# A first-layer matmul in place of an unread one, a weight load in two pieces, and the last output tile as 384 and 128 columns

## Chip, cores, metric

One core of one Trainium2 chip. The metric is the device time of one execution in microseconds. An execution is repeated several times on a chip, in rounds beside the kernel before; single executions of one kernel differ by 0.4 to 1.8 us within a set here (with two further outliers, 509.71 and 510.44), which is more than anything this change can do. In the profiles PE is TensorE (PEld its weight loads), DVE is VectorE, ACT ScalarE, POOL GpSimd and SP SyncE.

## The reference, cut to what matters

```python
# per batch (8) and head (8), sequence 1024, head size 64, projected to 64 rows
k_proj = einsum('ks,bhsd->bhkd', E, k);  v_proj = einsum('ks,bhsd->bhkd', F, v)
attn = softmax(q @ k_proj.T / sqrt(64)) @ v_proj
x = attn, heads side by side: (8192, 512)
h = x @ w_in                      # 512 -> 2048, "first layer"
g = h * clip(h + 3, 0, 6) / 6
out = g @ w_out                   # 2048 -> 512, "second layer"
```

## The kernel before

Only the parts that the change and the argument touch; `...` marks cuts.

```python
def busy(n):                       # matmuls on ones; nobody reads them
    ps = pmm()
    for _ in range(n):
        nc.tensor.matmul(ps, ones[:, :P], ones, start=True, stop=True)
busy(12)
...
for j in range(KO):                # first batch: k and q, then v, pair of heads by pair
    load_pair("k", j); load_q0(0, slice(2 * j, 2 * j + 2))
...
for j in range(KO):
    load_pair("v", j)
...                                # all of these are issued by GpSimd, one queue
for lo, n in ((0, 128), (128, 128), (256, 256), (512, 256), (768, 256),
              (1024, 512), (1536, 512)):
    load_w_in(lo, n)
load_q0(1, slice(0, H))
...                                # w_out in four quarters
load_kqv(1, "kvq")                 # the second batch
...
# end of First.first_block(), the first batch's first half
            self.vals(2, nc.vector.tensor_copy)
            products(1)
            busy(1)
            products(2)
            self.vals(3, nc.scalar.copy)   # project the last pair of v, copy out of PSUM
            busy(1)                        # unread, while ScalarE copies
            products(3)                    # values of the last pair, then xT on VectorE
...
two_groups(xT, 0, g[0], ((0, 1, 2), (3,)))   # first layer, groups 0 and 1
for fo in range(2, FO):
    first_group(xT, 0, g[0], fo)
...
two_groups(xT, 1, g[1], ((0, 1), (2, 3)))
for fo in range(2, FO):
    first_group(xT, 1, g[1], fo)
    pop()
    if fo == 7:
        second.projected()         # second batch: project k and v, matmuls taking turns
...
# second_group(): store of a finished row block
        o_sb = opool.tile([P, d_model], f32, tag="o_sb", name="o_sb")
        (copy or nc.scalar.copy)(o_sb, o_ps)
        nc.sync.dma_start(out=o_dst, in_=o_sb)
```

Each first-layer group is four matmuls of 512 columns (one for each quarter of the contraction), an ACTIVATE on ScalarE and a product on VectorE. The last output tile is cut in two halves of 256 columns, so that the first leaves while the second is computed.

The softmax here doesn't subtract the row's maximum and nothing guards it: scores larger than these inputs give would overflow.

## Time and profile before

| | kernel before |
|---|---|
| time, median of the first 3 runs | 507.60 us (507.38 to 507.77) |
| span of the profiled run | 505.97 us |
| last pair of v: PE starts its projection | 19.73 us, after a wait for the load |
| first product of the first layer on VectorE | 23.39 us |
| PE starts the last output tile | 499.02 us |
| from there to the end | 6.95 us |

Between the first product of the first layer and the last tile, the same instructions run in the same order in before and after. If one kernel is 0.4 us ahead at both points it has lost nothing in between, and if its lead shrinks, the place where it shrinks is a wait. I call the difference of the start of the same instruction in two kernels its **lead**. The lines of the profile stand in the prediction below.

### The profile page before, as it was taken

What the parts mean: (1) busy time and instruction counts of PE and PEld (TensorE: products, weight loads), DVE (VectorE), ACT (ScalarE), POOL (GpSimd) and SP (SyncE); (2) the same over time, 40 slices, a digit from 0 to 9 for tenths busy, and PEclk for the clock granted to TensorE, in tenths of its full rate; (3) what the DMA queues carried; (4) which work ended last, traced back from release to release, by engine and by line L of the source; (5) the groups of instructions that cost most, each with busy time, mean ns of one, the idle gap of its engine ahead of it and who ended that gap; (6) DMA issues with size and microseconds to landing.
All of it is one profiled execution on the core that took longest, in us unless ns stands there. A gap on an engine that the chain in (4) does not pass through costs nothing.

```text
span 506.0 us, 7034 instructions
## 1 busy us (share of the span) xinstructions
PE 495.5 (98%) x2729; PEld 225.1 (44%) x2779; DVE 245.1 (48%) x384; ACT 256.3 (51%) x438; POOL 37.9 (8%) x57
## 2 busy tenths in 40 slices
PE   8899999999999999999999999999999999999997
PEld 4444444444444444444444444444444444444444
DVE  3582736865733564536635455533752446334420
ACT  3656466567564444654555544654455544434431
POOL 8610020020020020010002000000000000000000
PEclk9999999999999999999999999999999999999999
DMA  9999999599299988699317990248110361101112
GB/s 166 199 205 207 202 157 234 109 149 199 79 152 193 264 149 172 137 159 251 113 43 134 216 263 26 63 97 209 41 43 32 79 162 43 41 22 42 43 42 84
DMA packets 77530, 66.04 MB, mean 131 GB/s; under 512 B 36200, under 2 KB 66664, under 8 KB 77496
## 3 DMA queue, kind: packets, MB, share of 16 engines
q0 software_dynamic: 31952, 29.36, 37.1%
q1 hardware_dynamic: 45320, 35.82, 27.0%
q10 hardware_dynamic: 224, 0.39, 0.3%
q8 instruction: 22, 0.36, 0.3%
q14 instruction: 12, 0.10, 0.1%
HBM read 69.73 MB, written 16.94 MB: 171 GB/s over the span
## 4 chain that ended last, share of the span: by engine, by line
PE 94%; DMA 2%; POOL 2%; issue 1%; ACT 1%; DVE 0%; ACTq 0%; POOLq 0%
PE mm L530 43%; PE mm L497 43%; PE at L195 2%; DMA v<-in_v_dram 2%; PE at L244 1%; PE at L226 1%; PE mm L244 1%; PE mm L522 1%; POOL q L106 1%; PE mm L264 1%; POOL k L110 1%; ACT aT L235 0%; PE mm L226 0%; POOL v L110 0%; PE mm L195 0%
## 5 line engine op out<-in xcount | busy, mean ns | idle before, releaser
L503 DVE SCALAR_TENSOR_TENSOR g<-r,mm 128x512 bf16<-128x512 f32 x256 | 173.6, 687 | 179.1 <-ACT r L502 178.3
L497 PE MATMUL mm<-xT,w_in_sb 128*128 128x512 bf16 x998 | 229.2, 379 | 1.5
L530 PE MATMUL mm<-w_out_sb,g 128*128 128x512 bf16 x985 | 227.8, 379 | 1.9 <-issue 1.0
L502 ACT ACTIVATE r<-mm 128x512 f32<-128x512 f32 x256 | 152.3, 599 | 74.5 <-PE mm L497 73.2
L497 PEld LDWEIGHTS <-w_in_sb 128*128 128x128 bf16 x1024 | 99.6, 98 | 121.8 <-issue 3.3
L530 PEld LDWEIGHTS <-g 128*128 128x128 bf16 x1008 | 96.7, 98 | 120.5 <-issue 7.4
L535 ACT COPY o_sb<-mm 128x512 f32<-128x512 f32 x55 | 32.3, 587 | 126.6 <-PE mm L530 126.6
L257 DVE TENSOR_TENSOR xT<-at,rec 128x512 bf16<-128x512 f32 x42 | 26.5, 682 | 6.5 <-ACT rec L176 6.5
L235 ACT ACTIVATE aT<-at 128x512 bf16<-128x512 f32 x38 | 20.2, 615 | 9.1 <-PE at L226 9.1
L201 DVE CAST kp<-at 64x512 bf16<-64x512 f32 x12 | 7.7, 677 | 15.5 <-PE at L195 15.5
L216 POOL COPY mark<-qT 1x1 bf16<-1x1 bf16 x4 | 0.7, 176 | 161.2 <-DMA qT<-q 161.2
L235 ACT ACTIVATE aT<-mm 128x512 bf16<-128x512 f32 x18 | 10.3, 613 | 3.6 <-PE mm L226 3.6
L535 DVE COPY o_sb<-mm 128x512 f32<-128x512 f32 x8 | 5.5, 688 | 13.4 <-PE mm L530 13.4
L195 PE MATMUL at<-k,e_t 128*64 128x512 bf16 x48 | 11.5, 382 | 0.0
L195 PE MATMUL at<-v,f_t 128*64 128x512 bf16 x48 | 11.5, 382 | 0.0
L257 DVE TENSOR_TENSOR xT<-mm,rec 128x512 bf16<-128x512 f32 x14 | 9.0, 685 | 4.3 <-PE mm L244 4.3
L176 ACT ACTIVATE rec<-rec 128x1024 f32<-128x1024 f32 x10 | 10.6, 1060 | 0.3
L170 ACT ACTIVATE rec<-mm 128x512 f32<-128x512 f32 x10 | 5.5, 595 | 7.9 <-PE mm L244 5.4
L170 ACT ACTIVATE few<-mm 128x512 f32<-128x512 f32 x10 | 5.4, 595 | 7.4 <-PE mm L264 7.4
L93 PE MATMUL mm<-ones 128*128 128x512 bf16 x18 | 7.4, 546 | 1.5 <-DVE halves L84 1.5
L204 DVE CAST vp<-at 64x512 bf16<-64x512 f32 x12 | 8.3, 694 | 0.4
L195 PEld LDWEIGHTS <-e_t 128*64 128x64 bf16 x56 | 5.6, 109 | 6.6 <-issue 1.9
(75 smaller groups left out, 160.5 us busy)
## 6 DMA issues: line engine op xcount, KB each, us to landing
out_dram<-o_sb SPq DMA_DIRECT2D x63, 256.0 KB, 2.5
rec<-rows SPq DMA_DIRECT2D x40, 256.0 KB, 6.3
k<-in_k_dram POOLq DMA_DIRECT2D x7, 1024.0 KB, 14.9
v<-in_v_dram POOLq DMA_DIRECT2D x7, 1024.0 KB, 20.7
q<-in_q_dram POOLq DMA_DIRECT2D x7, 1024.0 KB, 10.6
w_out_sb<-in_moe_w_out_dram POOLq DMA_DIRECT2D x4, 512.0 KB, 16.9
k<-in_k_dram POOLq DMA_DIRECT2D x4, 256.0 KB, 5.5
v<-in_v_dram POOLq DMA_DIRECT2D x4, 256.0 KB, 7.8
```

What stands on the lines that cost most here:

```text
L170: nc.scalar.activation(rec[:, i], den, AF.Ln)
L176: nc.scalar.activation(flat, flat, AF.Exp, scale=-1.0)
L195: nc.tensor.matmul(ps[e * KP:(e + 1) * KP], ef_t[e][:, so, :], kqv[self.b]["kv"[e]][:, :, so, :], start=(so == 0), stop=(so == SO - 1))
L204: nc.vector.tensor_copy(self.vp[a * KP:(a + 1) * KP], self.ps[KP:].rearrange("p (h d) -> p h d", d=D))
L235: nc.scalar.activation(self.aT[j][:, r].rearrange("p a n -> p (a n)"), tiles[r], AF.Exp, scale=scale)
L244: nc.tensor.matmul(tiles[t][c:c + D].rearrange("p (r n) -> p r n", r=2), stationary(r, 2 * j + a), self.aT[j][r:r + KP, :, a, :], start=Tr ...
L257: nc.vector.tensor_mul(self.xT[:, j, t, :], av[t], rec[:, t])
L497: nc.tensor.matmul(h_ps, w_in_sb[:, ko, fo * P:(fo + 1) * P], xT[:, ko, t, :], start=(ko == 0), stop=(ko == KO - 1))
L502: nc.scalar.activation(r, h_ps, AF.Relu, bias=0.5, scale=1.0 / 6.0)
L503: nc.vector.scalar_tensor_tensor(g[:, fo, :], r, 1.0, h_ps, op0=ALU.min, op1=ALU.mult)
L530: nc.tensor.matmul(o_ps, g[:, fo, c * P:(c + 1) * P], w_out_sb[:, fo, :], start=(fo == 0), stop=(fo == FO - 1))
L535: (copy or nc.scalar.copy)(o_sb, o_ps)
```

## The change

Intent: PE has a hole of half a microsecond while ScalarE copies the last pair of v, filled with an unread matmul. Let a matmul of the first layer do that duty. Load a later part of w_in in two pieces so that the earlier PE finds it there. At the end, make the piece that leaves last smaller.

```diff
-                  (1024, 512), (1536, 512)):
+                  (1024, 256), (1280, 256), (1536, 512)):
...
             self.vals(3, nc.scalar.copy)
-            busy(1)
+            meanwhile()
             products(3)
...
-            for e, copy, dma in ((0, nc.vector.tensor_copy, nc.sync), (1, nc.scalar.copy, nc.scalar)):
-                half = slice(e * d_model // 2, (e + 1) * d_model // 2)
+            most = d_model * 3 // 4
+            for piece, copy, dma in ((slice(0, most), nc.vector.tensor_copy, nc.sync),
+                                     (slice(most, d_model), nc.scalar.copy, nc.scalar)):
...
+    early = []
+    def meanwhile():
+        early.append(TwoGroups(xT, 0, g[0]))   # allocates the two PSUM tiles
+        early[0].part(0, (0,))                 # group 0, first quarter of the contraction
...
-    two_groups(xT, 0, g[0], ((0, 1, 2), (3,)))
+    early[0].part(0, (1, 2))
+    early[0].part(1, (0, 1, 2))
+    for fo in range(2):
+        early[0].part(fo, (3,))
+    early[0].out()
```

More of the change, by code (lines that the diff above doesn't have):

```diff
@@ L423, in values, with first_block @@
             return self.quads(lambda r, h: self.vp[r:r + KP, h, :], t, j, alloc)
-        def first_block(self):
+        def first_block(self, meanwhile):
             recs = {}
@@ L516, in second_group @@
         if (b, t, c) == (B - 1, NB - 1, SB - 1):
-            for e, copy, dma in ((0, nc.vector.tensor_copy, nc.sync), (1, nc.scalar.copy, nc.scalar)):
-                half = slice(e * d_model // 2, (e + 1) * d_model // 2)
-                o_ps = pmm()[:, :d_model // 2]
+            most = d_model * 3 // 4
+            for piece, copy, dma in ((slice(0, most), nc.vector.tensor_copy, nc.sync),
+                                     (slice(most, d_model), nc.scalar.copy, nc.scalar)):
+                n = piece.stop - piece.start
+                o_ps = pmm()[:, :n]
                 for fo in range(FO):
-                    nc.tensor.matmul(o_ps, g[:, fo, c * P:(c + 1) * P], w_out_sb[:, fo, half],
+                    nc.tensor.matmul(o_ps, g[:, fo, c * P:(c + 1) * P], w_out_sb[:, fo, piece],
                                      start=(fo == 0), stop=(fo == FO - 1))
-                o_sb = opool.tile([P, d_model], f32, tag="o_sb", name="o_sb")[:, :d_model // 2]
+                o_sb = opool.tile([P, d_model], f32, tag="o_sb", name="o_sb")[:, :n]
                 copy(o_sb, o_ps)
-                dma.dma_start(out=o_dst[:, half], in_=o_sb)
+                dma.dma_start(out=o_dst[:, piece], in_=o_sb)
             return
@@ L547, with __init__, part, parts @@
     first = First(xT)
-    first.first_block()
-    x_next = x_tile()
-    g = [g_tile(), g_tile()]
-    def two_groups(xT, t, g, kos):
-        tiles = [pmm(), pmm()]
-        for part in kos:
-            for fo in range(2):
-                h_part(tiles[fo], xT, t, fo, part)
-        for fo in range(2):
-            h_out(tiles[fo], g, fo)
-    two_groups(xT, 0, g[0], ((0, 1, 2), (3,)))
+    g = [g_tile(), g_tile()]
+    class TwoGroups:
+        def __init__(self, xT, t, g):
+            self.xT, self.t, self.g = xT, t, g
+            self.tiles = [pmm(), pmm()]
+        def part(self, fo, kos):
+            h_part(self.tiles[fo], self.xT, self.t, fo, kos)
+        def parts(self, *kos):
+            for some in kos:
+                for fo in range(2):
+                    self.part(fo, some)
+            self.out()
+        def out(self):
+            for fo in range(2):
+                h_out(self.tiles[fo], self.g, fo)
+    early = []
+    def meanwhile():
+        early.append(TwoGroups(xT, 0, g[0]))
+        early[0].part(0, (0,))
+    first.first_block(meanwhile)
+    x_next = x_tile()
+    early[0].part(0, (1, 2))
+    early[0].part(1, (0, 1, 2))
+    for fo in range(2):
+        early[0].part(fo, (3,))
+    early[0].out()
     for fo in range(2, FO):
@@ L579 @@
             (first.second_scores, first.second_sums, first.second_values)[i]()
-    two_groups(xT, 1, g[1], ((0, 1), (2, 3)))
+    TwoGroups(xT, 1, g[1]).parts((0, 1), (2, 3))
     for fo in range(2, FO):
@@ L644 @@
                     if fo == 0:
-                        two_groups(xT, t, g, ((0, 1, 2), (3,)))
+                        TwoGroups(xT, t, g).parts((0, 1, 2), (3,))
                 else:
```

## The prediction

> **What bounds the kernel now.** I read the page first (busy table and chain of waits by line), then the chain of waits in order of time for the first 45 us, then the timeline of 19.7 to 21.3 us and of the last 12 us, then the landings of the loads.
>
> ```profile
> span 506.0 us, 7034 instructions
> PE 495.5 (98%) x2729; PEld 225.1 (44%) x2779; DVE 245.1 (48%) x384; ACT 256.3 (51%) x438; POOL 37.9 (8%) x57
> PE 94%; DMA 2%; POOL 2%; issue 1%; ACT 1%; DVE 0%; ACTq 0%; POOLq 0%
> ```
>
> PE is busy in 98% of the span and is 94% of the chain that ended last. Between 60 us and the end, the view of the waits has for PE only these two:
>
> ```profile
> PE mm L530 <- issue: 1.0, 6, 0.2
> PE mm L530 <- DVE g L503: 0.2, 1, 0.2
> ```
>
> So behind the first stage the program is one row of matmuls that waits for nothing of weight: what is taken from PE's row early comes off the end, and a transfer that merely comes sooner is worth nothing. What can be won lies at the head, where PE waits for loads, in the number of matmuls, and behind the last matmul. The head, from the chain in order of time (start, duration, what):
>
> ```profile
> 9.70 9.99 DMA v<-in_v_dram
> 19.68 0.05 issue
> 19.73 0.63 PE at L382 x8
> 20.36 0.02 issue
> 20.39 0.27 ACT vp L385
> 20.66 0.04 issue
> 20.70 0.40 PE at L414 x2
> 21.11 10.25 PE mm L497 x47
> ```
>
> The last pair of the first batch's v lands; eight matmuls project it (L382), ScalarE copies it out of PSUM (L385), two matmuls multiply it with the attention weights (L414), and then the first layer of the MLP runs (L497). PE has a hole in this chain from the projection's end of issue (about 20.15) to 20.70, while ScalarE copies. In that hole stands now a matmul on ones that nobody reads; the timeline shows its weight load, and the product that finishes xT on VectorE:
>
> ```profile
> 20.13 0.10 PEld L93 LDWEIGHTS <-ones 128*128 128x128 bf16 x1
> 21.22 0.69 DVE L443 TENSOR_TENSOR xT<-at,o_sb 128x512 bf16<-128x512 f32 x1 [1.21 <-PE at L414]
> ```
>
> The tail, from the timeline (start, duration, engine, line, operation):
>
> ```profile
> 499.02 3.66 PE L522 MATMUL mm<-w_out_sb,g 128*128 128x256 bf16 x32
> 501.03 0.42 DVE L525 COPY o_sb<-mm 128x256 f32<-128x256 f32 x1 [14.30 <-PE mm L522]
> 501.48 0.33 SPq L526 DMA_DIRECT2D out_dram<-o_sb  x1
> 502.76 0.37 ACT L525 COPY o_sb<-mm 128x256 f32<-128x256 f32 x1 [2.91 <-PE mm L522]
> 503.16 0.35 ACTq L526 DMA_DIRECT2D out_dram<-o_sb  x1
> ```
>
> The first half leaves early and its landing (2.0 us after issue) is at 503.5; the second is issued at 503.16, lands 1.8 us later at 504.96, and about 1.0 us of closing follows to 506.0. So the end hangs on the second piece.
>
> **What the Trainium skill says.** (1) "TensorE: Matmul & The Clock Gate", Back-to-back issue gap: N/2.4 + 2.5 ns for an isolated stream, but about 81 ns for pairs of weight load and matmul at N=128. The trace sides with the first: sixteen L497 matmuls take 3.45 us in the chain, 216 ns each, and eight 128-column pairs at L382 take 0.62 us of which the last one's latency is 0.219, so (0.62 - 0.219)/7 = 57 ns. (2) "ScalarE: Activation LUTs", What ACT_TABLE_LOAD costs: 186 ns + 0.833 ns per column with immediate operands. The trace has 587 ns at 512 columns, 372 at 256 and 265 at 128: a slope of 0.84, on a base some 25 ns lower. (3) "DMA: Bandwidth & Descriptors", Issuing engines are not separate DMA queues: transfers issued from SP and ACT share the 16 DMA engines. Nothing in the tail shows this yet, since the two pieces hardly overlap there (503.5 against 503.16). (4) The same page, Anatomy of one DMA: a fixed part near 2 us that does not shrink with the size (stated for GpSimd's path). For stores from SP the trace has 2.5 us for 256 KB and 2.0 for 128 KB, so some 1.5 us fixed and 0.25 us per 64 KB.
>
> **Part 1, the early matmul.** It takes away one warm-up matmul (216 ns of PE) and puts one of the first layer's own (first tile, first quarter of the contraction) in its place; later the first layer has one matmul fewer to do. The hole is 0.55 us and either matmul fits in it, so the values still start at 20.70 and the first layer still at 21.04. **Gain: one matmul, 0.216 us**, if nothing that comes 0.22 us sooner then waits. I check each:
> - The first quarter of w_in (128 columns) is issued at 10.80 and lands 9.2 us later, at 20.0. It is needed at about 20.15 now, rather than at 21.04. It still fits if it starts by 20.48 (20.70 less 0.216).
> - The last product is on VectorE from 21.22 to 21.91. Six matmuls stood before the first that needs it (21.04 + 6 x 0.216 = 22.34); now five (22.12). It is still done.
> - w_in 128 to 255 lands at 11.57 + 9.2 = 20.8, needed at 21.5; columns 256 to 511 at 12.80 + 9.2 = 22.0, needed at 22.55; 512 at 23.3, needed at 24.3; 768 at 24.7, needed at 26.0; 1024 to 1535 at 16.06 + 11.2 = 27.26, needed at 21.04 + 31 x 0.216 = 27.7; 1536 at 17.32 + 12.5 = 29.8, needed at 31.2.
> - The first quarter of w_out lands at 20.84 + 14.2 = 35.04, needed at 35.70 - 0.22 = 35.48. The second batch's v: 27.56 + 26.9 = 54.5, needed at 55.28 - 0.22 = 55.06.
>
> No wait appears, the tightest margin being 0.15 us for the first piece of w_in (with 0.3 more before it costs anything).
>
> **Part 2, w_in in two pieces.** The same bytes, one more issue on GpSimd (0.74 us, on an engine 8% busy). The first half lands a good microsecond sooner (26.0 rather than 27.26), where PE doesn't wait before and would not wait after (27.7). GpSimd's issues wait for the eighth load before them, as the releasers show:
>
> ```profile
> POOL q L106 <- DMA v<-in_v_dram: 1.9, 1, 1.9
> POOL k L124 <- DMA w_in_sb<-in_moe_w_in_dram: 0.6, 1, 0.6
> ```
>
> so every load behind it is issued one landing later: the last of w_in at 19.96 instead of 17.32, w_out at about 21.6 instead of 20.84. The queue has some 10 us of data before it all the time, so landings should stay. Pieces of 256 columns came at 1.36 us each (22.0, 23.34, 24.72), those of 512 in 2.55: the split may cost 0.16 us of transfer, leaving w_out at 35.2 against 35.48. **Gain: 0**; it is insurance for part 1.
>
> **Part 3, the last tile.** PE: thirty-two matmuls of 256 columns run at (3.66 - 0.272)/31 = 109 ns, 3.5 us. Sixteen of 384 at an estimated 162 (between 109 and 216) and sixteen of 128 at 57 make 2.6 + 0.91 = 3.5: **the same**, and the last matmul still ends at about 502.68. Then ScalarE copies 128 columns in 265 ns rather than 372, which saves 0.107; its store has 64 KB instead of 128, an estimated 0.25 us less: issued at 503.06, it lands at 503.06 + 1.55 = 504.6. The other piece ends on PE at 499.02 + 15 x 0.162 + 0.33 = 501.78, is copied on VectorE from 501.89 for 0.556 us (425 at 256, 688 at 512, half way), issued at 502.48, and with 192 KB lands 2.25 us later, at 504.73. So both pieces now land nearly together, and the later of them 0.23 us before the old 504.96. They overlap on the same 16 engines for the last half microsecond, so I take **0.2 us**.
>
> **Sum:** 0.216 + 0 + 0.2 = 0.42 us; 507.6 - 0.42 = **507.2 us**.
>
> **Rivals.** (a) **The early matmul waits for w_in**, and since PE runs in order, the last pair's values wait behind it. For it: the margin is 0.15 us, and the landing before it jumped by 2.5 us where others of its size took 1.3. Against it: v and w_in come from one queue, so a late w_in mostly goes with a late v, and 0.3 us of the hole is free. If w_in were 0.5 us late, the gain of part 1 would be gone: 507.4. (b) **A later load takes the gain back.** For it: w_out has only 0.3 to 0.45 us left, and the split moves its issue back; against it: its queue is never empty. That too would leave the gain of part 3 alone, 507.4. (c) **The larger first piece becomes the last to land**, because 384 columns come out of PE and VectorE a microsecond later and both stores share the engines; then the tail gains 0 to 0.1, 507.3. If the 128-column matmuls ran at the skill's 81 ns, PE would lose 16 x 24 ns = 0.38 and the whole would stand at 507.5; L382 speaks against it. (d) **Nothing visible:** three runs of before span 0.39 us, about my whole gain.
>
> **Range and chances.** Everything lies between -0.1 and -0.7 us, to which the scatter of runs is added: 506.7 to 507.7. Two per cent would be 10 us, and no part touches that much: faster 0.3%, within 2% 99.2%, slower 0.5%.
>
> **What would show it.** Part 1: one warm-up matmul fewer at L93; a first-layer weight load near 20.13; values at 20.7 still; the first layer's second tile ending 0.2 us sooner; no PE wait for w_in. Part 2: eight issues of w_in, w_out issued later but landing about 35.1, no wait of PE at the first second-layer matmul. Part 3: PE's end 0.2 us sooner, ScalarE's copy near 265 ns, both stores landing within 0.2 us of each other. The prediction is wrong if the values start later than 20.9, if PE waits for w_out, if the 128-column matmuls are spaced by 80 ns, or if v itself lands at another time, which would move everything by as much.

## The result, and the profile after

| | before | after |
|---|---|---|
| time, median of 6 runs each, same rounds | 507.69 us (507.23 to 507.86) | 507.08 us (506.75 to 507.77) |
| span of the profiled run | 505.97 us | 505.29 us |

The ratio is 0.9991, with a 95% interval of 0.9978 to 1.0004. Ratios here are the mean time of one kernel's runs over that of the other's of the same rounds, so not quite the ratio of the medians. 12 runs of the changed kernel have a mean of 507.31 us and 37 runs of the kernel before 507.68 (one more, at 509.71, is left out). They come from several chips; the difference is 0.36 us, with a standard error of about 0.13 from the scatter of the runs.

So the number predicted, 507.2, held. The profile of the changed kernel, though, does not have the shape predicted. The page first:

```profile
span 505.3 us, 7033 instructions
PE 97%; ACT 1%; issue 1%; DVE 0%; ACTq 0%
```

The chain that ended last has no DMA any more: before, 2% of it was the landing of v. The timeline of the head (start, duration, engine, line, operation, wait before):

```profile
19.31 0.62 PE L382 MATMUL at<-v,f_t 128*128 128x128 bf16 x8
19.96 0.27 ACT L385 CAST vp<-at 128x128 bf16<-128x128 f32 x1 [0.58 <-PE at L382]
20.11 0.10 PEld L497 LDWEIGHTS <-w_in_sb 128*128 128x128 bf16 x1 [0.36 <-DMA w_in_sb<-in_moe_w_in_dram]
20.44 0.40 PE L414 MATMUL at<-aT,vp 64*64 64x512 bf16 x2 [0.51 <-ACT vp L385]
20.77 9.45 PE L497 MATMUL mm<-xT,w_in_sb 128*128 128x512 bf16 x43
```

The projection starts at 19.31 without a wait for v, 0.42 us sooner than before. The early matmul then waits for w_in until 20.11. ScalarE's copy is done at 20.23, but the values start only at 20.44, behind the early matmul. Before, they started 0.04 us after the copy. The first product of the first layer leads by 0.48 us (22.91 against 23.39): 0.42 from v, and no more than 0.06 from the early matmul that should have given 0.216.

The tail:

```profile
498.60 3.66 PE L524 MATMUL mm<-w_out_sb,g 128*128 128x384 bf16 x32
501.45 0.56 DVE L527 COPY o_sb<-mm 128x384 f32<-128x384 f32 x1 [15.15 <-PE mm L524]
502.04 0.33 SPq L528 DMA_DIRECT2D out_dram<-o_sb  x1
502.33 0.27 ACT L527 COPY o_sb<-mm 128x128 f32<-128x128 f32 x1 [2.91 <-PE mm L524]
502.63 0.35 ACTq L528 DMA_DIRECT2D out_dram<-o_sb  x1
```

PE needs the same 3.66 us, the two copies take 0.56 and 0.27 us as worked out, and the span ends 6.69 us after the tile's start rather than 6.95. The lead at the last tile is 0.42 us and not 0.48: 0.06 was lost on the way. Adding up: 0.42 + 0.06 - 0.06 + 0.26 = 0.68 us.

Three questions follow. Is v sooner by the change or by chance? What is the early matmul worth? Where are the 0.06 us lost?

### The profile page after: what moved, and what is told of

Read it like the earlier page. It is cut to its first block, busy times and chain, and to the rows that moved or that the text cites. A ratio compares the mean times of both kernels' runs of the same rounds, so it can differ in the third digit from the quotient of the medians. Undisturbed runs are those within 1.5% of the kernel's fastest.

```text
span 505.3 us, 7033 instructions
## 1 busy us (share of the span) xinstructions
PE 495.5 (98%) x2728; PEld 224.9 (45%) x2778; DVE 245.3 (49%) x384; ACT 256.2 (51%) x438; POOL 38.7 (8%) x58
## 4 chain that ended last, share of the span: by engine, by line
PE 97%; ACT 1%; issue 1%; DVE 0%; ACTq 0%
PE mm L532 43%; PE mm L497 43%; PE at L195 2%; PE mm L93 1%; PE at L244 1%; PE at L226 1%; PE mm L244 1%; PE mm L524 1%; PE mm L264 1%; PE at L414 1%; ACT aT L235 0%; PE mm L226 0%; PE at L382 0%; PE at L394 0%; PE mm L195 0%
## 5 line engine op out<-in xcount | busy, mean ns | idle before, releaser
L503 DVE SCALAR_TENSOR_TENSOR g<-r,mm 128x512 bf16<-128x512 f32 x256 | 173.6, 687 | 178.9 <-ACT r L502 178.1
L502 ACT ACTIVATE r<-mm 128x512 f32<-128x512 f32 x256 | 152.3, 599 | 74.5 <-PE mm L497 73.2
L204 DVE CAST vp<-at 64x512 bf16<-64x512 f32 x12 | 8.3, 694 | 0.4
```

The lines of the kernel that those rows point to most:

```text
L502: nc.scalar.activation(r, h_ps, AF.Relu, bias=0.5, scale=1.0 / 6.0)
L503: nc.vector.scalar_tensor_tensor(g[:, fo, :], r, 1.0, h_ps, op0=ALU.min, op1=ALU.mult)
```

## The experiments

Theory: two gates stand in the head, both of them landings. The first is the last pair of v of the first batch, early or late by chance (which of the two, in one execution, I call its draw), with w_in's first piece right behind it. The second is the second batch's v near 55 us. Part 1 gains only as far as neither closes. Rivals: the split of w_in brought v forward; the early matmul is worth its 0.216 us everywhere; the loss near 55 us is something else.

All traces together, in us. "Fetch" is the time of the only 16 KB instruction load of the first 30 us. "v out" is the GpSimd issue that waits for the landing of v's last pair. P is the start of that pair's projection on PE, G1 the first product of the first layer. "Lost" is how much longer the step from the 23rd to the 25th product (around the second batch's projection) took than the 3.68 us it needs without a wait (not given where the projection was moved). T is the start of the last tile.

| kernel | fetch | v out | P | G1 | G1-P | lost | T | span | end-T |
|---|---|---|---|---|---|---|---|---|---|
| before | 17.61 | 19.96 | 19.73 | 23.39 | 3.66 | 0 | 499.02 | 505.97 | 6.95 |
| b_again (before, again) | 18.19 | 18.60 | 19.24 | 22.90 | 3.66 | 0.50 | 499.06 | 505.99 | 6.93 |
| t_only | 17.50 | 19.93 | 19.69 | 23.35 | 3.66 | 0 | 498.98 | 505.61 | 6.63 |
| s_only | 17.69 | 20.15 | 19.91 | 23.58 | 3.67 | 0 | 499.21 | 506.20 | 6.99 |
| e_only | 17.58 | 19.99 | 19.75 | 23.20 | 3.45 | 0 | 498.82 | 505.76 | 6.94 |
| after | 17.84 | 18.51 | 19.31 | 22.91 | 3.60 | 0.06 | 498.60 | 505.29 | 6.69 |
| a_again (after, again) | 18.00 | 18.54 | 19.20 | 22.96 | 3.76 | 0.22 | 498.80 | 505.49 | 6.69 |
| fetch_late | 17.31 | 19.70 | 19.46 | 22.90 | 3.44 | 0.06 | 498.59 | 505.29 | 6.70 |
| proj8 | 17.67 | 20.00 | 19.76 | 23.21 | 3.45 | - | 499.10 | 505.79 | 6.69 |
| best | 17.64 | 20.34 | 20.11 | 23.38 | 3.27 | - | 499.27 | 506.0 | 6.7 |
| few_warm | 19.58 | 18.60 | 20.61 | 24.05 | 3.44 | 0 | 499.68 | 506.36 | 6.68 |
| late_stores | 17.47 | 18.75 | 18.91 | 22.71 | 3.80 | 0 | 498.34 | 505.23 | 6.89 |
| few_late | 18.52 | 18.97 | 19.41 | 23.48 | 4.07 | 0 | 499.11 | 505.99 | 6.88 |
| held_stores | 17.55 | 18.30 | 19.07 | 22.58 | 3.51 | 0 | 498.21 | 504.9 | 6.7 |

### The kernel before, again

> The kernel before, unchanged, a second time: a null comparison and a second profile. Question: in the first profile of before, the last pair of v landed at 19.65 us, about 1.3 us later than the rhythm of the three pieces before it (14.5, 15.8, 17.1); in the profile of the changed kernel it landed near 18.2 and PE did not wait for it. Theory A (chance: a 16 KB instruction fetch falls on one of the DMA engines at 17.6 us and catches the last packets of v, or not): here the landing may lie at either place, the ratio is 1.000 within 0.001, and the span goes with it (505.7 if v is on time, 506.0 if late). Theory B (the split of w_in brought v forward): here v lands at 19.6 again.

Edit: none. Measured 507.66 us against 507.80, ratio 0.9995 (0.9982 to 1.0008). This nearly answers the first and the third question. GpSimd's issue that waits for v, in the first profile of before:

```profile
19.96 0.88 POOL L106 DMA_DIRECT2D q<-in_q_dram  x1 [1.90 <-DMA v<-in_v_dram]
```

and in the second one, with PE's projection and the start of the first layer:

```profile
18.60 0.88 POOL L106 DMA_DIRECT2D q<-in_q_dram  x1 [0.50 <-DMA v<-in_v_dram]
19.24 0.62 PE L382 MATMUL at<-v,f_t 128*128 128x128 bf16 x8
20.55 0.61 PE L497 MATMUL mm<-xT,w_in_sb 128*128 128x512 bf16 x2
```

The same kernel has v 1.4 us sooner, does not wait for it, and leads by 0.49 us at the first product: all that the changed kernel had there, without the change. Yet its span is 505.99, as before. The lead is lost at the second batch's projection, whose matmuls take k and v in turn:

```profile
54.82 0.40 PE L195 MATMUL at<-k,e_t 128*64 128x512 bf16 x1
55.34 0.38 PE L195 MATMUL at<-v,f_t 128*64 128x512 bf16 x1
55.35 0.11 PEld L195 LDWEIGHTS <-e_t 128*64 128x64 bf16 x1 [0.42 <-issue]
```

The first matmul on k starts at 54.82 and the first on v only at 55.34. The loads' landing confirms it: v was issued at 27.73 and landed 27.6 us later, at 55.3. The wait view names no DMA for it ("issue"), so the gap has to be read from the starts. That is the second gate.

### One part at a time

> Only the early matmul; w_in in its old pieces, the last tile in halves. Theory of the prediction: 0.216 us shorter than before (ratio 0.9996). Rival, from the changed kernel's profile: if v is on time, the early matmul waits for the first piece of w_in (landing near 20.1) and the last pair's values wait behind it, so that the gain is only about 0.05 us (ratio 0.9999); if v is late, at 19.65, the gain is the whole 0.216. The time may not resolve this; the profile shows which it is: values starting at 20.44 with the early matmul at 20.11, or 0.04 us behind the copy.

Edit: the change without the split and with the last tile in halves. 507.53 us against 507.80, ratio 0.9992 (0.9979 to 1.0006); the time does not resolve it. Here v was late:

```profile
19.75 0.62 PE L382 MATMUL at<-v,f_t 128*128 128x128 bf16 x8 [0.48 <-DMA v<-in_v_dram]
20.15 0.10 PEld L497 LDWEIGHTS <-w_in_sb 128*128 128x128 bf16 x1
20.73 0.40 PE L414 MATMUL at<-aT,vp 64*64 64x512 bf16 x2 [0.36 <-ACT vp L385]
```

The early matmul finds w_in, the values follow the copy at once, and G1-P is 3.45 us rather than 3.66: the whole matmul is gained, as predicted. The lead of 0.19 us is unchanged at the last tile (0.20). In column G1-P, v late gives 3.44 or 3.45 with the early matmul (three profiles); v on time gives 3.51 to 3.80 with it in after, a_again, late_stores and held_stores, against 3.66 without it (in one profile, b_again). So **with v on time the early matmul is worth between +0.15 and -0.14 us** in these four, by when w_in's first piece lands (the matmul started at 19.79 us in the best of them); few_late, where it started only at 20.68, widens that to -0.41, and few_warm, where nothing waited for w_in, to +0.22. The matmul that waits holds the values behind it (in after, ScalarE's copy was done at 20.23 and the values started at 20.44). With v's pair and w_in in the old order, w_in's first piece lands between 19.7 and 20.6 whether v came at 18.3 or 19.65 (few_warm, 19.05, is the exception); v's chance does not move it along.

> Only the last tile as 384 and 128 columns. Theory of the prediction: PE takes the same 3.66 us for the 32 matmuls, ScalarE's copy falls from 372 to 265 ns, and the span ends 0.2 us sooner after the last matmul (3.3 us from the last PE end to the end of the span before). From the changed kernel's profile: 0.27 to 0.3 us. Ratio 0.9994 to 0.9996. Rival: the larger first piece lands last; then under 0.1.

Edit: only the last tile. 507.46 us against 507.80, ratio 0.9992 (0.9979 to 1.0005). From the last tile's start to the end are 6.63 us here and 6.68 to 6.70 in the other profiles with this tile and all stores on SP and ScalarE; with halves it is 6.93 to 6.99. Between the means, 6.95 and 6.68, that is a gain of 0.27 us. The issues of the last stores (last column: us to landing):

```profile
out_dram<-o_sb SPq DMA_DIRECT2D x1, 192.0 KB, 1.9
out_dram<-o_sb ACTq DMA_DIRECT2D x1, 64.0 KB, 1.6
```

SP's piece, issued at 502.42, lands at 504.3; ScalarE's, issued at 503.01, at 504.6. The larger piece does not land last.

> Only w_in's columns 1024 to 1535 in two pieces. Theory of the prediction: nothing, ratio 1.0000, PE waits for no load of w_in or w_out, and the loads behind it land where they did. Theory B: v's last pair lands near 18.2 instead of 19.65, and the first layer starts about 0.3 us sooner, ratio 0.9994.

Edit: only the split. 507.95 us against 507.80, ratio 0.9999 (0.9983 to 1.0015).

```profile
20.15 0.74 POOL L129 DMA_DIRECT2D w_in_sb<-in_moe_w_in_dram  x1 [1.49 <-DMA v<-in_v_dram]
```

v is late again. The split does not bring it forward, and with b_again that rival has fallen from both sides. PE waits for no later piece of w_in, here or in e_only without the split: where v is late, the split gains and costs nothing. Without the split and with v on time there is only b_again, and there the undivided piece lands at 27.44 us and is just too late: its first weight load starts at 27.48, and the lead falls from 0.48 to 0.46 us. So what the split is worth as insurance, with v on time and the early matmul, no run here tests.

> The changed kernel, unchanged, a second time. If two gates set the head (the last pair of the first batch's v near 18.3 or 19.7 us by chance, then the second batch's v at 54.5 to 55.3), the tail alone is worth the same 0.30 us everywhere, the early matmul 0.2 us where v is late and under 0.1 where it is on time, and up to all of that is lost where the second batch's v lands after 54.8. Ratio to before 0.9988 to 0.9996; the last tile begins at 498.5 to 498.9 and the span ends 6.65 us after that.

Edit: none to the changed kernel. 507.38 us against 507.69, ratio 0.9992 (0.9977 to 1.0007). v was on time, the early matmul waited for w_in until 20.17, and the second batch's v landed at 55.0 and cost 0.22 us. What is left at the last tile is 0.22 us plus the tail. So in both profiles of the changed kernel the lead at the end comes from v's draw, and the early matmul had 0.06 us and -0.10 of its 0.216.

### What makes v late

The traces hold one load of 16384 bytes of instructions in this stage. The DMA view of 17.6 to 18.6 us, in before (queue, packets, MB, share):

```profile
q8 instruction: 1, 0.02, 5.9%
```

A share of 5.9% of 16 engines over this 1 us is 0.94 us of one engine, and the load comes when PE has some 246 to 266 records behind it. The Trainium skill ("Runtime: NRT & Kernel Launch", Instruction fetch mechanics) says that instructions are refilled in blocks of 16 KiB, 256 instructions, and that crossing a boundary is "mostly hidden". The count agrees here; "hidden" is put in doubt by one load that comes late behind it in every profile, as the count below shows.

> The changed kernel with its twelve warm-up matmuls at the start replaced by six in f32 on the same bytes (about as long, some 18 PE instructions fewer). Theory (the 16 KB instruction fetch comes when PE has run some 250 instructions, at 17.5 to 18.2 us in the six profiles, and holds up one DMA engine by about a microsecond; v's last pair was late in the four with the fetch at or before 17.69 and on time in the two with 17.84 and 18.19): the fetch moves to 18.3 or later, v's last pair is on time (no wait of PE for it), and the first layer starts near 20.7. Rival (the fetch has nothing to do with v): the fetch moves or not, v lands at 19.7 in spite of it. The time gains nothing if the second batch's v then holds PE up at 54.8 to 55.3.

Edit:

```diff
-    busy(12)
+    wide = ones.bitcast(f32)
+    ps = pmm()[:, :TOK // 2]
+    for _ in range(6):
+        nc.tensor.matmul(ps, wide[:, :P], wide, start=True, stop=True)
```

507.21 us against 507.69, ratio 0.9988 (0.9973 to 1.0002). The experiment missed: each f32 matmul ran as two, so the trace has twelve weight loads and twelve matmuls as before, and the fetch did not move to later in PE's row. PE's first stages merely ran about 0.4 us sooner than in after, the fetch came at 17.31, and v was late. It tells nothing against the theory and shows only that the trace must be asked whether an edit did what it was meant to.

> The changed kernel with ten unread matmuls fewer on PE before 13 us (seven warm-ups at the start rather than twelve, and the two and three small ones later left out), so twenty PE instructions fewer. Nothing of it is on the path. Theory (the 16 KB fetch comes when PE has run about 250 instructions; in the ten profiles so far v's last pair was late in all seven with the fetch at 17.31 to 17.69 us and on time in all three with 17.84 to 18.19): the fetch moves by most of a microsecond, to 18.4 or later, v is on time and PE does not wait for it. Rival (chance alone decides, or the fetch is not tied to PE's count): the fetch stays at 17.5 to 18.0, or v is late although it moved. A third outcome: the clock falls because PE is idle more; then the head is longer. The early matmul may still wait for the first piece of w_in, which then is the one in flight.

Edit: `busy(12)` to `busy(7)`, `busy(2)` and the three `busy(1)` of the key stage left out. 508.16 us against 507.67, ratio 1.0009 (0.9997 to 1.0021). The fetch came at 19.58, again after 246 PE records, so it is tied to PE's count. v was on time and, as in no other kernel with v on time, w_in's first piece too: GpSimd did not wait for it at 19.34, and G1-P is the full 3.44. But PE paid for it. The timeline of PE's first projection of keys, in before:

```profile
7.83 0.63 PE L366 MATMUL at<-k,e_t 128*64 128x128 bf16 x8
```

and with few warm-up matmuls:

```profile
8.14 1.06 PE L365 MATMUL at<-k,e_t 128*64 128x128 bf16 x8 [0.52 <-DVE e_t L151]
```

The eight take 1.06 us instead of 0.63, and groups like them are back at their usual times only from 13.6 us. The unread matmuls are unread, not useless.

So one piece behind the fetch comes late, by 0.5 to 1.4 us against the rhythm of the pieces around it. Of the fourteen profiles it is v in seven, all with the fetch at 17.69 or before; in the others, among them all five with 17.84 or later, it is w_in's first piece, or in few_warm its third (2.2 us after the second, where other profiles have 1.2 to 1.3). Whichever it is, it lands 2.0 to 2.5 us after the fetch began, in all fourteen, although the fetch itself lies anywhere from 17.31 to 19.58: the delay goes with the fetch. That the fetch causes it is likely by this, and not shown, since no edit moved the fetch and nothing else. Two with the fetch at 17.47 and 17.55 had v on time and w_in late instead, so the moment alone does not decide which piece it is; which engine the load falls on and how far that engine is I cannot see in these views. This stays open.

### What the second gate costs, and what opens it

> The changed kernel with the second batch's projection one group of the first layer later (0.86 us later for that v). Theory (the second batch's v is a second gate): PE never waits inside the projection, the lead or lag of the first layer at 23 us is the same as at 59 us and at the last tile, to 0.02 us beyond the moved group. Rival (the loss came from something else at 55 us): a loss of 0.06 or more appears again. Time: equal to the changed kernel or up to 0.3 us less.

Edit: `if fo == 7:` to `if fo == 8:` for the second batch's projection. 507.56 us against 507.69, ratio 0.9992 (0.9979 to 1.0005). PE no longer waits in the projection, but 0.26 us are lost elsewhere, so my expectation fell. VectorE's copy of projected values (L204) and the first scores on PE (L226), in before:

```profile
66.45 0.69 DVE L204 CAST vp<-at 64x512 bf16<-64x512 f32 x1
68.45 0.47 PE L226 MATMUL mm<-qT,kT 64*64 64x256 bf16 x8
```

and with the later projection:

```profile
67.14 0.69 DVE L204 CAST vp<-at 64x512 bf16<-64x512 f32 x1
67.86 1.28 DVE L503 SCALAR_TENSOR_TENSOR g<-r,mm 128x512 bf16<-128x512 f32 x2
68.27 0.74 PE L226 MATMUL mm<-qT,kT 64*64 64x256 bf16 x8
```

The later projection moves VectorE's copy one product (L503) back, so the product that starts at 67.86 now ends at 68.55 instead of 68.47, although PE is 0.18 us ahead. By the trace's semaphores it frees a PSUM tile that the scores write next: their second matmul starts at 68.60 (68.52 before), right behind it, and the scores are strung out. The transposed queries are not what PE waits for: SP's transposes end 0.46 us later than before, but at 67.3, 0.9 us ahead of the scores. So there is a third gate behind the second, a PSUM tile that VectorE frees, and this edit itself closed it.

> All together: the later fetch, the projection one group later, w_in's first 128 columns queued ahead of the last pair of v, and a second unread matmul (between the products of pairs 1 and 2) replaced by one of the first layer. Theory: both early matmuls find their w_in, PE does not wait for v, the first group of the first layer is 0.3 to 0.5 us ahead of the changed kernel's (first product of the gate at 22.5 us rather than 22.9), nothing takes it back at 55 us; span about 504.8 us, ratio to before 0.9976 to 0.9984. Rival: the queue shifts and v's last pair now lands after 19.3, so that PE waits for it and the lead is under 0.2.

Edit: fetch_late and proj8 together, w_in's first 128 columns queued ahead of v's last pair, and a second early matmul. 507.88 us against 507.69, ratio 1.0001 (0.9987 to 1.0015): it falls.

```profile
20.11 0.62 PE L387 MATMUL at<-v,f_t 128*128 128x128 bf16 x8 [0.92 <-DMA v<-in_v_dram]
```

Both early matmuls find w_in, but v is now behind it and behind the fetch too, and its wait of 0.92 us eats both. The rival is what came. The third gate of proj8 takes another 0.26 us (a lead of 0.01 us at the first product, -0.25 at the last tile).

> The changed kernel with the first three output stores (768 KB, issued at 47.4 to 49 us on SP) issued from GpSimd instead, where they queue behind the second batch's q. Theory (the second gate is the second batch's v, and the loads there are short of bandwidth): v lands up to 3 us sooner, at 51.5 to 53, PE never waits inside the second projection, and the lead over the kernel before at 54.7 us is still there at 59 us and at the last tile (lost there so far: 0.06, 0.21 and 0.06 us with the change, 0.50 in the second profile of before). Rival: the stores run beside the loads at no cost to them; v lands at 54.5 to 55.3 as before. Time: 0 to 0.2 us less than the changed kernel.

Edit:

```diff
-        nc.sync.dma_start(out=o_dst, in_=o_sb)
+        queue = nc.gpsimd if (b, t) == (0, 0) and c < SB - 1 else nc.sync
+        queue.dma_start(out=o_dst, in_=o_sb)
```

507.58 us against 507.67, ratio 0.9997 (0.9984 to 1.0010). The second batch's v lands at 27.25 + 25.8 = 53.0 us, where it had landed between 54.5 and 55.3 with the stores in their old place (53.9 in few_warm, where PE and so the stores were later), and the lead of 0.68 us at 54.5 us is still 0.68 at the last tile. So the first stores hold up v: in the three kernels without them at that place it lands at 52.7 to 53.2. But end-T grows by 0.2 us (6.89, and 6.88 in few_late, the only other kernel with stores on GpSimd). The stores of the tail are not it: the last one lands 1.6 us after its issue, as elsewhere. From that landing to the end are 1.24 and 1.22 us in these two, and 1.02 to 1.04 in the other twelve; what the close waits for, the trace does not name.

> Both. If the two gates are what takes the gain back, this is the fastest: v on time and no wait at the second projection, the last tile beginning at 498.3 to 498.6, span 505.0 to 505.2, ratio to before 0.998 to 0.9986. If not, it stands where the changed kernel does.

Edit: those of few_warm and late_stores together. 508.48 us against 507.67, ratio 1.0021 (1.0007 to 1.0034): far inside the 2%, but the only interval of all that leaves out 1, and on the slow side, so the expectation fell. The fetch came at 18.52 and w_in's first piece late behind it (the early matmul waited until 20.68; G1-P is 4.07). The slow PE of few_warm was over by about 11 us here. The profiled execution was the fastest of its six, and as long as before's (505.99 us), so what made the others slower its trace does not show. The second gate was open here too.

> The changed kernel with the same first three output stores left on SP, but behind the transposes of the second batch's keys and queries in SP's order, so that they go out at about 60 us rather than 47 to 49. Theory (the stores take bandwidth from the second batch's v, which is the second gate; in the run with the stores on GpSimd v landed at 53.1 us instead of 54.9 and nothing was lost at 55 us, but the close of the program grew from 6.68 to 6.88 us after the last tile began): v lands at 53 to 54, PE does not wait inside the second projection, nothing is lost between 54.7 and 59 us, and the close is 6.68 us again. Span: the lead of the first layer (0.4 to 0.7 us by the draw of the first gate) plus 0.27 below 505.97, so 505.0 to 505.3; ratio to before 0.998 to 0.999, and to the changed kernel 0 to 0.2 us less. Rival: the stores, now beside the second batch's query transposes and the third batch's loads, hold up the first scores near 68 us, and the loss comes back there.

Edit: the three stores kept in a list and issued on SP behind the transposes of the second batch's queries.

```diff
-        nc.sync.dma_start(out=o_dst, in_=o_sb)
+        if (b, t) == (0, 0) and c < SB - 1:
+            held.append(lambda: nc.sync.dma_start(out=o_dst, in_=o_sb))
+        else:
+            nc.sync.dma_start(out=o_dst, in_=o_sb)
...
+            while held:            # in turn(), after the transposes
+                held.pop(0)()
```

507.23 us (506.68 to 507.58) against 507.56, ratio 0.9992 (0.9979 to 1.0006).

```profile
54.46 0.40 PE L196 MATMUL at<-k,e_t 128*64 128x512 bf16 x1
54.47 0.40 PE L196 MATMUL at<-v,f_t 128*64 128x512 bf16 x1
```

v, at 26.97 + 25.8 = 52.8 us, is there long before PE; k and v start together; the lead of 0.81 us at the first product is 0.81 at the last tile, and the close has its 6.7 us again. The span, 504.9 us, is the shortest of all fourteen profiles. Part of that is a good draw at the first gate, and the profiled execution was the fastest of its five. In the times it cannot be told from the changed kernel (507.31 mean of 12 runs), so it is shown to open the second gate, and not shown to be faster.

## Why the prediction was right, and where it was not

- **The sum, 507.2 us: right.** 507.08 in the rounds of the result, 0.36 us of gain over all runs against 0.42 predicted. No part was near 2%. That it is so near is in part luck: the times (0.36, standard error 0.13) cannot tell 0.42 from the 0.27 of the tail alone, and in the two profiles of the changed kernel the early matmul gave +0.06 and -0.10 us of its 0.216. Of the prediction's own signs of being wrong, v did land at another time; of its signs of being right, PE did wait for w_in, and the last stores landed 0.36 us apart (503.89 and 504.25) rather than within 0.2.
- **Part 1, "Gain: one matmul, 0.216 us": right in size, where v is late** (G1-P 3.44 and 3.45 against 3.66). The step that failed is the check of w_in's first piece, "needed at about 20.15 now". It took from one profile that v lands at 19.65. v is on time in seven of fourteen profiles; then the piece is needed some 0.4 us sooner, at 19.7, and still lands at about 20 (in all of the seven but few_warm). Then rival (a) is what happens, at +0.06 and -0.10 us in the two profiles of the changed kernel. The argument against that rival, "a late w_in mostly goes with a late v", had it the wrong way round: it needed w_in to be early when v is, and it is not.
- **"What is taken from PE's row early comes off the end": right up to some tenths of a microsecond, and then wrong.** The view of waits named no load behind the first stage because PE happened to arrive at 55.27, after the second batch's v at 54.5. That margin was in my list (needed 55.06, landing 54.5), but as a fixed number. The landing scatters from 54.5 to 55.3 with the stores in their old place and PE at its usual time, and took back 0.50, 0.22, 0.06 and 0.06 us in four profiles. Rival (b) had the right mechanism and the wrong load: I named w_out, for which PE waited nowhere.
- **Part 2, "Gain: 0": right where v is late.** s_only and e_only show it from both sides. The check of the undivided piece, landing at 27.26 and needed at 27.7, was again made for a late v: with v on time it cost 0.02 us in b_again. The insurance itself stays untested.
- **Part 3, 0.2 us: right mechanism, two terms mis-sized.** PE's time and both copies were as worked out. The 192 KB store was set at 2.25 us and took 1.8 to 1.9; so it is not the last to land. The 64 KB store, set at 1.55, took 1.6, which is 0.16 us less than the 128 KB one (1.76 to 1.81) rather than 0.25; with the 0.107 of ScalarE's copy that is the gain of 0.27 us. The 128-column matmuls keep up with their weight loads: 32 matmuls take 3.66 us in either cut, and rival (c) falls with its 0.38 us.
- **What the profile after seemed to show**, 0.68 us, is mostly the draw of v: read by itself it would have credited the change with 0.42 us that b_again has without it.

## What to carry to other kernels

A profile is one draw: before a few tenths of a microsecond are credited to an edit, take the unchanged kernel's profile a second time and follow the lead of the same instruction from stage to stage. When PE is made to arrive earlier, each load that landed just in time before is the next bound, even if the view of waits does not name it; list the margins, and ask by how much the landings scatter. Work placed in a hole of an in-order engine must have its inputs sooner than the hole opens in the best case, not in the one case seen.

## What the Trainium skill lacked or had wrong

- "TensorE: Matmul & The Clock Gate", Back-to-back issue gap: it gives 81 ns (128 columns) and 131 ns (512 columns) as sustained spacing of weight-load and matmul pairs. Here pairs ran at 57 and 216 ns, the values it calls isolated, and a tile with sixteen 128-column pairs took no longer than one without (3.66 us both).
- "Runtime: NRT & Kernel Launch", Instruction fetch mechanics: the refill is called mostly hidden. Here a 16 KB refill took 0.9 to 1.0 us of one DMA engine, and one load behind it, of v or of w_in, came 0.5 to 1.4 us late in each of fourteen profiles; PE waited for that load in twelve of them. No page speaks of what a refill does to loads in flight.
- "DMA: Bandwidth & Descriptors", Anatomy of one DMA: a fixed part near 2 us is given for GpSimd's path, and none for a whole store from SP or ScalarE. Stores of 64 KB from ScalarE landed in 1.6 us and of 192 KB from SP in 1.8 to 1.9. No page says how far the landing of a queued load scatters between executions: 0.9 us here (54.5 to 55.3) for a load issued 27 us before.
- "ScalarE: Activation LUTs", What ACT_TABLE_LOAD costs: its 186 ns + 0.833 ns a column is for ACTIVATE with immediate operands and makes an estimated 613 ns at 512 columns; those of L502 took 599. The prediction set it against ScalarE's copies, for which the page has no figure of its own: they have the same slope (0.84) and took 587 ns, some 25 less.
